# A 2:4-pruned matmul on one Trainium2 core: another opening, with six weight pieces, two load queues and bf16 transposes

## The chip, the core and the metric

The kernel runs on one NeuronCore of a Trainium2 chip. Five engines work side by side, each with its own instruction stream, and wait for one another by semaphores: TensorE (matmuls and their weight loads; PE and PEld in the profile), VectorE (DVE), ScalarE (ACT), GpSimd (POOL) and SyncE (SP). Here SyncE and ScalarE issue the DMAs, each on a queue of its own; the profile counts such issues under SPq and ACTq. Matmul results go to PSUM, which has eight banks, and are read out by VectorE or ScalarE.

The metric is device microseconds of one execution, lowest is best. Before the change the median of 13 runs is 237.35 us.

## What is computed

```python
B, S, D = 16, 512, 1024          # x: (B, S, D), w: (D, D), b: (D), all bf16

def reference(x, w, b):
    N, M = 2, 4
    wg = w.reshape(D // M, M, D)
    mag = jnp.abs(wg)
    order = jnp.argsort(mag, 1)
    thr = jnp.take_along_axis(mag, order[:, M - N:M - N + 1, :], 1)
    wp = (wg * (mag >= thr)).reshape(D, D)
    return jnp.einsum("bsd,df->bsf", x, wp) + b
```

Of every four neighbouring rows of `w`, in each column, the two largest in magnitude are kept and the others set to zero. The pruned matrix then multiplies 8192 tokens of 1024 features, and a bias is added. The product takes 64 token tiles x 8 slices of 128 features x 2 halves of 512 output columns: 1024 matmuls of 128 x 128 by 128 x 512.

## The kernel before

**Two parts.** The first seven token tiles (0 to 6) are multiplied in the "packed" part, while the weights are still being loaded and pruned. The other 57 tiles follow in the "natural" part.

**Packed part.** `w` is held with four neighbouring rows side by side in one partition (`wv`, "(g q m) f -> q g m f"): group g is one half of the 1024 rows, q the partition, m the row of the four. Pruning then compares values of the same partition. The weights are loaded and pruned in seven pieces (L123), given as group and columns: two of 128 columns, three of 256, two of 512. For each piece VectorE runs abs, hi and lo (the larger and smaller of two pairs), t1 and t2, thr (the second largest), mask and mult (`do`, L161); for some pieces ScalarE takes the abs (L159). The product of mult goes to `wp`.

The token tiles must be transposed in the same packed order. `transpose(t, g)` (L192) does this on TensorE for one group ("a" is group 0, "b" group 1): it takes pairs of bf16 values as one fp32 word, so two fp32 transposes move four slices; the identity is fp32. The result lies in PSUM (`psum_t`, two buffers) and `copy_xt` (L201) brings it to SBUF on ScalarE. `mm_piece(t, i)` (L209) multiplies tile t by piece i with four matmuls, m = 0 to 3, into the accumulator of tile t and output half h.

Accumulators come from `psum_o`, six buffers that are handed out in turn; the first goes to the fillers, which are matmuls of zeros into an unused tile (`filler`, L129). When the first output half of a tile is complete, `stage` (L224) copies it to SBUF on ScalarE and so frees its buffer; the second half stays in PSUM until `finish(t)` (L229) adds the bias to both halves on VectorE and issues the store.

**Order.** The order of the packed part is written out by hand as three strings, one for each engine (L249). A token is an operation: T3a transposes tile 3, group 0; C3a copies it; M3.1 multiplies tile 3 by piece 1; F2 is two fillers of 128 columns; S3 stages tile 3; W5 saves piece 5; `abs0` to `mult6` are pruning steps. `run` (L306) emits tokens as soon as what `needs` names has been emitted; each engine then executes its string in order. Ahead of the strings there are six fillers of 512 columns and three of 128.

**Loads.** All loads stand ahead on SyncE's queue, in this order: w of piece 0 and 1 (256 columns, 256 KB), x of tile 0, of tile 1, of tiles 2-3 (group 0; 128 KB for each tile), w of piece 2, x of tiles 4-5, w of piece 3, and so on up to the two 512 KB pieces and the bias.

**Natural part.** The pruned pieces are saved to DRAM (`save`, L183) and read back in natural row order (`reload`, L186) into `wp_nat`. The remaining tokens are loaded in batches by a transposing DMA (`load_batch`, L237). Batch 0 (five tiles) runs all first halves and then all second halves through `nat_group` (L332, matmuls of L334); the other batches interleave the halves (L369). `evac` (L337) adds the bias and `store` (L340) sends the tile out. On SyncE's queue the order after the loads is: four saves, batch 0, reload of half 0, reload of half 1, batches 1 and 2; the saves of the two 512-column pieces are on ScalarE's queue (W5, W6).

Of the kernel before, what the change touches and what calls it, by code (L numbers as in the profile page):

```python
# [10 lines left out]
def kernel(  # L11
# [7 lines left out]
    nc = tc.nc  # L19
    P = 128  # L20
    bf16 = mybir.dt.bfloat16
# [11 lines left out]
    FH = 512  # L33
# [13 lines left out]

    const = ctx.enter_context(tc.tile_pool(name="const", bufs=1))
    dram = ctx.enter_context(tc.tile_pool(name="dram", bufs=1, space=bass.MemoryType.DRAM))
    wtmp = ctx.enter_context(tc.tile_pool(name="wtmp", bufs=2))  # L50
    xtp = ctx.enter_context(tc.tile_pool(name="xtp", bufs=NPK))
    stg = ctx.enter_context(tc.tile_pool(name="stg", bufs=NPK))
    xtb = ctx.enter_context(tc.tile_pool(name="xtb", bufs=3))
# [13 lines left out]
    def pe(i):  # L67
        return seq("pe", i)

    def dve(i):  # L70
        return seq("dve", i)

    def act(i):
        return seq("act", i)
# [3 lines left out]

    zeros = const.tile([P, P], bf16)
    dve(nc.vector.memset(zeros[:], 0.0))  # L80
    spark = const.tile([P, 1], bf16)


    w_sb = const.tile([P, G, 4, Dout], bf16)
# [9 lines left out]
    def load_w(g, c0, c1, eng="sp"):  # L94
        issue(eng, w_sb[:, g, :, c0:c1], wv[:, g, :, c0:c1])

    def load_x(ta, tb, g, eng="sp"):
        xs = const.tile([P, tb - ta, HK], bf16, name=f"x_{ta}_{g}")
        issue(eng, xs[:], xv[:, ta:tb, g * HK:(g + 1) * HK])
        for t in range(ta, tb):  # L100
            x_sb[(t, g)] = xs[:, t - ta, :]


    act(nc.scalar.activation(spark[:], zeros[:, :1], Act.Abs))
    load_w(0, 0, CW)
    load_x(0, 1, 0)
    load_x(1, 2, 0)
    load_x(2, 4, 0)
    load_w(0, CW, FH)
    load_x(4, 6, 0)  # L110
    load_w(1, 0, CW)
    load_x(0, 2, 1)
    load_x(2, 4, 1)
    load_x(6, 7, 0)
    load_w(1, CW, FH)
    load_x(4, 6, 1)
    load_x(6, 7, 1)
    load_w(0, FH, Dout)
    load_w(1, FH, Dout)
    sp(nc.sync.dma_start(bias_sb[:], b.partition_broadcast(P)))  # L120


    pieces = [(0, 0, P), (0, P, CW), (0, CW, FH), (1, 0, CW), (1, CW, FH), (0, FH, Dout), (1, FH, Dout)]  # L123

    ident = const.tile([P, P], fp32)
    make_identity(nc, ident[:])
    warm_ps = psum_o.tile([P, FH], fp32, name="ps")

    def filler(n, rep=1):  # L129
        for _ in range(n):  # L130
            pe(nc.tensor.matmul(warm_ps[:, :rep * P], lhsT=zeros[:],  # L131
                                rhs=zeros[:, None, :].to_broadcast([P, rep, P]), start=True, stop=True))
# [6 lines left out]

    class Piece:  # L140


        def __init__(self, i):
            self.g, self.c0, self.c1 = pieces[i]
            n = self.n = self.c1 - self.c0
            self.w = w_sb[:, self.g, :, self.c0:self.c1]
            self.mag = wtmp.tile([P, 4, FH], bf16, name="mag", bufs=5)[:, :, :n]
            self.hi = wtmp.tile([P, 2, FH], bf16, name="hi")[:, :, :n]
            self.lo = wtmp.tile([P, 2, FH], bf16, name="lo")[:, :, :n]
            self.t1 = wtmp.tile([P, FH], bf16, name="t1")[:, :n]  # L150
            self.t2 = wtmp.tile([P, FH], bf16, name="t2")[:, :n]
            self.thr = wtmp.tile([P, FH], bf16, name="thr")[:, :n]
            self.mask = wtmp.tile([P, 4, FH], bf16, name="mask")[:, :, :n]

        def tt(self, out, a, b_, op):
            dve(nc.vector.tensor_tensor(out, a, b_, op=op))  # L156

        def abs_act(self):
            act(nc.scalar.activation(self.mag, self.w, Act.Abs))  # L159

        def do(self, *steps):  # L161
            magv = self.mag.rearrange("p (a j) f -> p a j f", j=2)
            for step in steps:
                if step == "abs":
                    dve(nc.vector.tensor_single_scalar(
                        self.mag.bitcast(u16), self.w.bitcast(u16), 0x7FFF, op=Alu.bitwise_and))
                elif step == "hi":
                    self.tt(self.hi, magv[:, :, 0, :], magv[:, :, 1, :], Alu.max)
                elif step == "lo":
                    self.tt(self.lo, magv[:, :, 0, :], magv[:, :, 1, :], Alu.min)  # L170
                elif step == "t1":
                    self.tt(self.t1, self.hi[:, 0, :], self.hi[:, 1, :], Alu.min)
                elif step == "t2":
                    self.tt(self.t2, self.lo[:, 0, :], self.lo[:, 1, :], Alu.max)
                elif step == "thr":
                    self.tt(self.thr, self.t1, self.t2, Alu.max)
                elif step == "mask":
                    self.tt(self.mask, self.mag,
                            self.thr[:, None, :].to_broadcast([P, 4, self.n]), Alu.is_ge)
                else:  # L180
                    self.tt(wp[:, self.g, :, self.c0:self.c1], self.w, self.mask, Alu.mult)

    def save(g, c0, c1, eng="sp"):  # L183
        issue(eng, scr_pk[:, g, :, c0:c1], wp[:, g, :, c0:c1])
# [7 lines left out]
    def transpose(t, g):  # L192


        xg = x_sb[(t, g)].bitcast(fp32).rearrange("p (q u) -> p u q", u=2)
        tp = psum_t.tile([P, 2, P], fp32, name="tp")
        for u in range(2):
            pe(nc.tensor.transpose(tp[:, u, :], xg[:, u, :], ident[:]))  # L198
        xpk[(t, g)] = tp

    def copy_xt(t, g):  # L201
        xt = xtp.tile([P, 2, P], fp32, name=f"xt{g}")
        act(nc.scalar.copy(xt[:], xpk[(t, g)][:]))  # L203
        v = xt[:].bitcast(bf16).rearrange("p u (t v) -> p u v t", v=2)
        xpk[(t, g)] = [v[:, m // 2, m % 2, :] for m in range(4)]

    ps_open = {}

    def mm_piece(t, i):  # L209
        g, c0, c1 = pieces[i]  # L210
        h = c0 // FH
        new = (t, h) not in ps_open
        if new:
            ps_open[(t, h)] = psum_o.tile([P, FH], fp32, name="ps")
        ps = ps_open[(t, h)]
        for m in range(4):
            pe(nc.tensor.matmul(ps[:, c0 - h * FH:c1 - h * FH], lhsT=xpk[(t, g)][m],  # L217
                                rhs=wp[:, g, m, c0:c1],
                                start=(new and m == 0), stop=(g == 1 and m == 3),
                                skip_group_check=True))  # L220

    staged = {}
# [14 lines left out]
    def load_batch(bi):  # L237
# [5 lines left out]
        for j in range(nb):  # L243
# [4 lines left out]

    order = {  # L249
        "pe": (  # L250
            "T0a T1a F2 T2a T3a F2 M0.0 M1.0 M2.0 M3.0 T4a T5a M0.1 M1.1 M2.1 M3.1 M4.0 M4.1 T0b "
            "T1b M5.0 M5.1 T2b T6a M0.2 T3b M1.2 M2.2 T4b M3.2 T5b T6b M4.2 M5.2 M0.3 M1.3 M2.3 "
            "M3.3 M4.3 M5.3 M0.4 M1.4 M2.4 M3.4 M4.4 M5.4 M6.0 M6.1 M6.2 M6.3 M6.4 M0.5 M1.5 M2.5 "
            "M3.5 M4.5 M5.5 M0.6 M1.6 M2.6 M3.6 M4.6 M5.6 M6.5 M6.6"
        ),
        "dve": (
            "abs0 hi0 lo0 t10 t20 hi1 thr0 lo1 mask0 t11 mult0 t21 thr1 mask1 mult1 abs2 hi2 lo2 "
            "t12 t22 thr2 mask2 mult2 hi3 lo3 t13 t23 thr3 mask3 mult3 hi4 lo4 t14 t24 thr4 mask4 "
            "mult4 hi5 lo5 t15 t25 thr5 mask5 mult5 hi6 lo6 t16 t26 thr6 mask6 mult6"
        ),  # L260
        "act": (
            "abs1 C0a C1a C2a C3a C4a C5a abs3 C0b C1b C2b C6a abs4 C3b C4b C5b C6b abs5 abs6 S0 S1 "
            "S2 S3 S4 S5 W5 S6 W6"
        ),
    }
    written = set()
    p = {}

    def needs(eng, tok):

        if tok[0] == "C":
            return ["T" + tok[1:]]
        if tok[0] in "TF":
            return []
        if tok[0] == "M":
            t, i = tok[1:].split(".")
            return [f"C{t}{'ab'[pieces[int(i)][0]]}", f"mult{i}"]
        if tok[0] == "S":
            return [f"M{tok[1:]}.{i}" for i in range(5)]
        if tok[0] == "W":  # L280
            return ["mult" + tok[1:]]
        return ["abs" + tok[-1]] if tok[:-1] in ("hi", "mask") else []

    def emit(eng, tok):
        if tok[0] == "T":
            transpose(int(tok[1]), "ab".index(tok[2]))
        elif tok[0] == "F":
            filler(int(tok[1:]))
        elif tok[0] == "C":
            copy_xt(int(tok[1]), "ab".index(tok[2]))  # L290
        elif tok[0] == "M":
            mm_piece(*map(int, tok[1:].split(".")))
        elif tok[0] == "S":
            stage(int(tok[1:]))
        elif tok[0] == "W":
            save(*pieces[int(tok[1:])], eng="act")
        else:
            i = int(tok[-1])
            if i not in p:
                p[i] = Piece(i)  # L300
            if eng == "act":
                p[i].abs_act()
            else:
                p[i].do(tok[:-1])

    def run(queues):  # L306
        while any(queues.values()):
# [6 lines left out]
            assert moved, queues  # L314

    filler(6, 4)
    filler(3)
    run({eng: order[eng].split() for eng in order})
    save(0, 0, CW)
    save(0, CW, FH)  # L320
    save(1, 0, CW)
    save(1, CW, FH)
    load_batch(0)
    reload(0)
    reload(1)
    load_batch(1)
    load_batch(2)
    for t in range(NPK):
        finish(t)


# [76 lines left out]
```

## Time and profile before

| | us |
|---|---|
| median of 13 runs | 237.35 (236.06 to 238.44) |
| the profiled execution, whole | 237.1 |
| its span, first to last instruction | 235.3 |
| TensorE matmuls busy (PE) | 229.6 (98%) |
| weight loads busy (PEld, beside PE) | 113.5 (48%) |
| VectorE busy | 104.8 (45%) |
| ScalarE busy | 16.0 (7%) |
| natural part, interleaved batches (L369) | 175.4 |
| packed products (L217) | 26.3 |
| batch 0 and the last tile (L334) | 21.0 |
| transposes (L198) | 6.1 |

How to read it: a line "L217 PE MATMUL ps<-wp,xt ... x84 | 10.0, 273 | 0.0" is a group of instructions of source line 217, with what they write and read, their number, busy time in us, mean duration of one in ns, and the engine's idle time just before them. Matmuls are pipelined, so the duration of one is longer than the distance to the next; the chain and the records of single instructions give the distance. In the chain of waits a line is a start, a duration (us) and what took it. A row of the table of stages has the granted clock of TensorE as the share of full speed, third from the end.

Landings of the first loads, from the records of single DMAs (issue start, landing, in us):

| load | issued | landed |
|---|---|---|
| w, group 0, columns 0-255 | 0.73 | 3.78 |
| x tile 0, group 0 | 1.48 | 4.10 |
| x tile 1, group 0 | 2.13 | 5.62 |
| x tiles 2-3, group 0 | 2.59 | 6.45 |
| w, group 0, columns 256-511 | 3.07 | 7.30 |
| x tiles 4-5, group 0 | 3.68 | 8.10 |
| w, group 1, columns 0-255 | 4.34 | 9.24 |

### The profile page before, as it was taken

How to read it: one execution, taken by the hardware profiler on the slowest of the kernel's cores; microseconds unless marked ns; L12 is line 12 of the kernel's file. 1: busy time of each engine (PE TensorE's matmuls, PEld its weight loads, DVE VectorE, ACT ScalarE, POOL GpSimd, SP SyncE). 2: the span in 40 equal slices, each digit the busy share in tenths (PEclk: the TensorE clock that was granted, in tenths of full speed). 3: DMA queues.
4: the chain of work that ended last, by engine and by line, in shares of the span. 5: the costliest groups of instructions: out<-in, count | busy, mean ns of one | idle time of the engine just before them, and what ended most of it. 6: DMA issues, size and time to landing. Idle time of an engine off the chain costs nothing.

```text
span 235.3 us, 2830 instructions
## 1 busy us (share of the span) xinstructions
PE 229.6 (98%) x1145; PEld 113.5 (48%) x1165; DVE 104.8 (45%) x182; ACT 16.0 (7%) x28; POOL 0.7 (0%) x6
## 2 busy tenths in 40 slices
PE   6999999999999999999999999999999999999995
PEld 2999444444444444444444444444444444444443
DVE  3899797433433432442443343244234334424424
ACT  4488000000000000000000000000000000000000
POOL 1000000000000000000000000000000000000000
PEclk9999999999999999999999999999999999999999
DMA  4999979999999822893219912497221221222122
GB/s 151 322 350 181 330 247 281 317 280 261 315 240 240 239 92 89 183 286 112 77 59 257 277 47 89 101 254 224 92 84 51 89 89 47 89 89 85 52 89 89
DMA packets 79500, 40.29 MB, mean 171 GB/s; under 512 B 60416, under 2 KB 71936, under 8 KB 79488
## 3 DMA queue, kind: packets, MB, share of 16 engines
q1 hardware_dynamic: 68352, 22.45, 42.4%
q10 hardware_dynamic: 11136, 17.67, 20.9%
q8 instruction: 9, 0.15, 0.3%
q14 instruction: 3, 0.02, 0.0%
HBM read 6.29 MB, written 18.87 MB: 107 GB/s over the span
## 4 chain that ended last, share of the span: by engine, by line
PE 96%; DMA 1%; issue 1%; SPq 1%; DVE 0%
PE ps L369 74%; PE ps L217 11%; PE ps L334 9%; PE tp L198 2%; DMA x<-in_x_dram 1%; SPq L92 1%; PE ps L131 0%; DVE o L338 0%
## 5 line engine op out<-in xcount | busy, mean ns | idle before, releaser
L369 PE MATMUL ps<-wp_nat,xb 128*128 128x512 bf16 x800 | 175.4, 379 | 0.8
L338 DVE TENSOR_TENSOR o<-ps,bias_sb 128x512 bf16<-128x512 f32 (+1 forms) x116 | 74.3, 678 | 120.5 <-PE ps L369 106.4
L369 PEld LDWEIGHTS <-xb 128*128 128x128 bf16 x816 | 79.8, 98 | 96.3
L217 PE MATMUL ps<-wp,xt 128*128 128x256 bf16 (+2 forms) x194 | 26.3, 294 | 0.1
L217 PEld LDWEIGHTS <-xt 128*128 128x128 bf16 x196 | 17.9, 102 | 7.3
L334 PE MATMUL ps<-wp_nat,xb 128*128 128x512 bf16 (+2 forms) x110 | 21.0, 348 | 0.1
L334 PEld LDWEIGHTS <-xb 128*128 128x128 bf16 x112 | 10.3, 98 | 10.7
L198 PE MATMUL tp<-ident,x 128*128 128x128 f32 x28 | 6.1, 339 | 1.0 <-DMA x<-in_x_dram 0.9
L159 ACT ACTIVATE mag<-w_sb 128x1024 bf16<-128x1024 bf16 (+2 forms) x5 | 6.5, 1317 | 1.6 <-DMA w_sb<-in_w_dram 1.6
L231 DVE TENSOR_TENSOR o<-ps,bias_sb 128x512 bf16<-128x512 f32 x7 | 4.8, 684 | 1.9 <-PE ps L217 1.9
L156 DVE TENSOR_TENSOR wp<-w_sb,mask 128x1024 bf16<-128x1024 bf16 (+2 forms) x7 | 5.4, 768 | 0.2
L156 DVE TENSOR_TENSOR mask<-mag,thr 128x1024 bf16<-128x1024 bf16 (+2 forms) x7 | 5.4, 768 | 0.2
L198 PEld LDWEIGHTS tp<-ident,x 128*128 128x128 f32 x28 | 4.4, 207 | 1.9 <-DMA x<-in_x_dram 1.1
L203 ACT COPY xt<-tp 128x256 f32<-128x256 f32 x14 | 4.9, 375 | 5.1 <-PE tp L198 5.1
L131 PE MATMUL ps<-zeros 128*128 128x128 bf16 (+1 forms) x13 | 3.9, 459 | 1.0 <-DVE zeros L80 1.0
L232 DVE TENSOR_TENSOR o<-st,bias_sb 128x512 bf16<-128x512 f32 x7 | 4.8, 681 | 0.0
L156 DVE TENSOR_TENSOR hi<-mag 128x512 bf16<-128x512 bf16 (+2 forms) x7 | 3.2, 461 | 1.4 <-ACT mag L159 1.4
L226 ACT COPY st<-ps 128x512 f32<-128x512 f32 x7 | 3.6, 608 | 0.9 <-PE ps L217 0.9
L156 DVE TENSOR_TENSOR lo<-mag 128x512 bf16<-128x512 bf16 (+2 forms) x7 | 3.2, 457 | 0.0
L131 PEld LDWEIGHTS <-zeros 128*128 128x128 bf16 x13 | 1.7, 143 | 2.8 <-issue 1.7
L156 DVE TENSOR_TENSOR thr<-t,t 128x256 bf16<-128x256 bf16 (+2 forms) x7 | 2.2, 310 | 0.2
L156 DVE TENSOR_TENSOR t<-hi 128x256 bf16<-128x256 bf16 (+2 forms) x7 | 2.1, 305 | 0.0
(11 smaller groups left out, 5.3 us busy)
## 6 DMA issues: line engine op xcount, KB each, us to landing
out_dram<-o ACTq DMA_DIRECT2D x58, 256.0 KB, 3.2
wp_nat<-wp_scratch SPq DMA_DIRECT2D x2, 1024.0 KB, 7.2
x<-in_x_dram SPq DMA_DIRECT2D x5, 256.0 KB, 5.1
out_dram<-o ACTq DMA_DIRECT2D x10, 128.0 KB, 1.7
w_sb<-in_w_dram SPq DMA_DIRECT2D x4, 256.0 KB, 4.6
w_sb<-in_w_dram SPq DMA_DIRECT2D x2, 512.0 KB, 7.2
wp_scratch<-wp SPq DMA_DIRECT2D x4, 256.0 KB, 7.6
wp_scratch<-wp ACTq DMA_DIRECT2D x2, 512.0 KB, 5.4
```

Of the source, the lines that this page charges most:

```text
L131: pe(nc.tensor.matmul(warm_ps[:, :rep * P], lhsT=zeros[:], rhs=zeros[:, None, :].to_broadcast([P, rep, P]), start=True, stop=True))
L156: dve(nc.vector.tensor_tensor(out, a, b_, op=op))
L159: act(nc.scalar.activation(self.mag, self.w, Act.Abs))
L198: pe(nc.tensor.transpose(tp[:, u, :], xg[:, u, :], ident[:]))
L203: act(nc.scalar.copy(xt[:], xpk[(t, g)][:]))
L217: pe(nc.tensor.matmul(ps[:, c0 - h * FH:c1 - h * FH], lhsT=xpk[(t, g)][m], rhs=wp[:, g, m, c0:c1], start=(new and m == 0), stop=(g == 1 an ...
L226: act(nc.scalar.copy(st[:], ps_open.pop((t, 0))[:]))
L231: dve(nc.vector.tensor_tensor(o[:, FH:], ps_open.pop((t, 1))[:], bias_sb[:, FH:], op=Alu.add))
L232: dve(nc.vector.tensor_tensor(o[:, :FH], staged.pop(t)[:], bias_sb[:, :FH], op=Alu.add))
L334: pe(nc.tensor.matmul(ps, lhsT=xt[:, kt, :], rhs=wp_nat[:, kt, c0:c1], start=(kt == 0), stop=(kt == KT - 1)))
L338: dve(nc.vector.tensor_tensor(o[:, c0:c1], ps, bias_sb[:, c0:c1], op=Alu.add))
L369: pe(nc.tensor.matmul(pss[h][:], lhsT=xt[:, kt, :], rhs=wp_nat[:, kt, h * FH:(h + 1) * FH], start=(kt == 0), stop=(kt == KT - 1)))
```

## The change

- **Pieces.** Six instead of seven: four of 256 columns and two of 512. The two 128-column pieces are one piece, 0. Its mask and mult, and its products, are split by rows: "y" is m = 2, 3 and "x" is m = 0, 1, and y goes first.
- **Loads.** The table-loading activation on ScalarE runs three times on 128 columns. Then ScalarE's queue issues x (group 0) of tile 6 and of tiles 4-5. SyncE's queue starts with the first weight piece, then x of tiles 2-3, the second piece, tile 6's group 1, and the rest in a new order, with tile 0's group 0 last but one among x and w.
- **Transposes.** Four bf16 transposes for a block instead of two fp32 ones; the identity is bf16; the copy still moves 256 words of 32 bits to a partition.
- **Pruning in place.** t1, t2, thr and mask overwrite hi, lo and mag, and every piece has its own buffers.
- **Order.** New strings: eight 128-column fillers ahead instead of three, F5, F6 and F7 between the first five transposes, tiles in the order 5, 4, 6, 2, 3, 1, 0, the last products M5.5 to M3.5. `needs` names more. The finishes follow in the order 2, 0, 3, 1, 6, 5, 4. The saves of the 512-column pieces (W5, W4) stand at the end of ScalarE's string.

```diff
-    spark = const.tile([P, 1], bf16)
+    spark = const.tile([P, P], bf16)
...
-    act(nc.scalar.activation(spark[:], zeros[:, :1], Act.Abs))
-    load_w(0, 0, CW)
+    load_w(0, 0, 256)
+    for _ in range(3):
+        act(nc.scalar.activation(spark[:], zeros[:], Act.Abs))
+    load_x(6, 7, 0, "act")
+    load_x(4, 6, 0, "act")
+    load_x(2, 4, 0)
+    load_w(0, 256, 512)
+    load_x(6, 7, 1)
+    load_x(1, 2, 0)
+    load_w(1, 256, 512)
+    load_x(2, 4, 1)
+    load_w(1, 0, 256)
+    load_x(4, 6, 1)
+    load_w(0, 512, 1024)
+    load_x(0, 2, 1)
     load_x(0, 1, 0)
-    load_x(1, 2, 0)
-    load_x(2, 4, 0)
-    load_w(0, CW, FH)
...
+    load_w(1, 512, 1024)
...
-    pieces = [(0, 0, P), (0, P, CW), (0, CW, FH), (1, 0, CW), (1, CW, FH), (0, FH, Dout), (1, FH, Dout)]
-
-    ident = const.tile([P, P], fp32)
+    pieces = [(0, 0, 256), (0, 256, 512), (1, 0, 256), (1, 256, 512), (0, 512, 1024), (1, 512, 1024)]
+
+    ident = const.tile([P, P], bf16)
...
+            elif step == "mask":
+                self.tt(self.mag[:, ms, :], self.mag[:, ms, :],
+                        thr[:, None, :].to_broadcast([P, n, self.n]), Alu.is_ge)
+            else:
+                self.tt(wp[:, self.g, ms, self.c0:self.c1], self.w[:, ms, :], self.mag[:, ms, :], Alu.mult)
...
-        xg = x_sb[(t, g)].bitcast(fp32).rearrange("p (q u) -> p u q", u=2)
-        tp = psum_t.tile([P, 2, P], fp32, name="tp")
-        for u in range(2):
-            pe(nc.tensor.transpose(tp[:, u, :], xg[:, u, :], ident[:]))
+        xg = x_sb[(t, g)].rearrange("p (q m) -> p m q", m=4)
+        tp = psum_t.tile([P, 4, P], bf16, name="tp")
+        for m in range(4):
+            pe(nc.tensor.transpose(tp[:, m, :], xg[:, m, :], ident[:]))
...
-        xt = xtp.tile([P, 2, P], fp32, name=f"xt{g}")
-        act(nc.scalar.copy(xt[:], xpk[(t, g)][:]))
+        xt = xtp.tile([P, 4, P], bf16, name=f"xt{g}")
+        act(nc.scalar.copy(xt[:].bitcast(fp32), xpk[(t, g)][:].bitcast(fp32)))
...
         "pe": (
-            "T0a T1a F2 T2a T3a F2 M0.0 M1.0 M2.0 M3.0 T4a T5a M0.1 M1.1 M2.1 M3.1 M4.0 M4.1 T0b "
-            "T1b M5.0 M5.1 T2b T6a M0.2 T3b M1.2 M2.2 T4b M3.2 T5b T6b M4.2 M5.2 M0.3 M1.3 M2.3 "
-            "M3.3 M4.3 M5.3 M0.4 M1.4 M2.4 M3.4 M4.4 M5.4 M6.0 M6.1 M6.2 M6.3 M6.4 M0.5 M1.5 M2.5 "
-            "M3.5 M4.5 M5.5 M0.6 M1.6 M2.6 M3.6 M4.6 M5.6 M6.5 M6.6"
+            "T6a F5 T5a T4a F6 T3a T2a F7 M5.0y M4.0y M6.0y M2.0y M5.0x M3.0x T6b T1a M6.0x M3.0y "
+            "M4.0x M2.0x M1.0y M1.0x T3b T2b M6.1 M4.1 M3.1 T4b M1.1 M5.1 T5b M2.1 M6.3 M3.3 M4.3 "
+            "T1b T0b M5.3 M2.3 M1.3 M3.2 M6.2 M5.2 T0a M4.2 M2.2 M1.2 M0.0y M0.1 M0.2 M0.3 M0.0x "
+            "M2.4 M3.4 M1.4 M0.4 M5.4 M4.4 M5.5 M2.5 M1.5 M4.5 M6.4 M0.5 M6.5 M3.5"
         ),
         "dve": (
...
+            "abs0 hi0 lo0 t10 t20 thr0 mask0y mask0x mult0y abs1 mult0x hi1 lo1 t11 t21 thr1 mask1 "
+            "mult1 lo3 hi3 t23 t13 thr3 mask3 mult3 lo2 hi2 t22 t12 thr2 mask2 mult2 lo4 hi4 t24 "
+            "t14 thr4 mask4 mult4 hi5 lo5 t25 t15 thr5 mask5 mult5"
         ),
         "act": (
-            "abs1 C0a C1a C2a C3a C4a C5a abs3 C0b C1b C2b C6a abs4 C3b C4b C5b C6b abs5 abs6 S0 S1 "
-            "S2 S3 S4 S5 W5 S6 W6"
+            "C6a C5a C4a C2a C3a C6b C1a abs3 C3b abs2 C2b C4b C5b abs4 C1b abs5 C0a S5 C0b S1 S4 "
+            "S6 S2 S0 S3 W5 W4"
...
-    filler(3)
+    filler(8)
...
-    for t in range(NPK):
+    for t in (2, 0, 3, 1, 6, 5, 4):
         finish(t)
```

## The prediction

> **What bounds the kernel now.** I read the chain of waits first, as shares and then in order of time up to 15 us, to see which engine sets the end and where it does not.
>
> ```profile
> PE 96%; DMA 1%; issue 1%; SPq 1%; DVE 0%
> PE ps L369 74%; PE ps L217 11%; PE ps L334 9%; PE tp L198 2%; DMA x<-in_x_dram 1%; SPq L92 1%; PE ps L131 0%; DVE o L338 0%
> ...
> 2.13 3.48 DMA x<-in_x_dram
> 5.62 0.04 issue
> 5.66 0.70 PE tp L198 x2
> 6.36 0.21 PE ps L131 x2
> ...
> 7.89 1.71 PE ps L217 x16
> 9.60 0.54 PE tp L198 x4
> 10.14 1.34 PE ps L217 x24
> ```
>
> From 5.66 us to the last matmul (the records of single instructions put its end at 232.64) TensorE never stops for more than 0.05 us. Whatever is not TensorE work from there on is hidden. The end can move in three ways: dense work starts at another time than 5.66, the dense stretch holds other work or a new stall, or its beginning runs at another speed. The last is visible above: 16 matmuls of 128 columns take 1.71 us (107 ns each), and later 24 of them take 1.34 us (56 ns). The groups of TensorE by form, up to 36 us, say the same:
>
> ```profile
> L217 PE MATMUL ps<-wp,xt 128*128 128x512 bf16 x54 | 12.1, 379 | 0.1
> L217 PE MATMUL ps<-wp,xt 128*128 128x256 bf16 x84 | 10.0, 273 | 0.0
> L198 PE MATMUL tp<-ident,x 128*128 128x128 f32 x28 | 6.1, 339 | 1.0 <-DMA x<-in_x_dram 0.9
> L131 PE MATMUL ps<-zeros 128*128 128x512 bf16 x6 | 2.7, 630 | 1.0 <-DVE zeros L80 1.0
> ```
>
> A 512-column filler at the start takes 630 ns, a 512-column matmul later 379. The table of stages gives a granted clock of 1.00 in every microsecond, so its first microseconds must not be trusted: the clock's records begin at 9.67 us, and there the spacing halves. I read it as half speed up to 9.67 us. Dense TensorE work had by then run for 4.0 us; before that it had stood still from 4.05 to 4.24 and from 4.91 to 5.66.
>
> Last, VectorE's row for a 256-column piece, since the change makes such a piece the first:
>
> ```profile
> 7.47 0.42 DVE L165 TENSOR_SCALAR mag<-w_sb 128x1024 uint16<-128x1024 uint16 x1
> ...
> 9.45 0.69 DVE L156 TENSOR_TENSOR mask<-mag,thr 128x1024 bf16<-128x1024 bf16 x1
> 10.17 0.69 DVE L156 TENSOR_TENSOR wp<-w_sb,mask 128x1024 bf16<-128x1024 bf16 x1
> ```
>
> **The unit of account.** At 9.98 us the kernel has six transposed blocks and 16 short matmuls (0.89 us at 56 ns) behind it, and 232.64 - 9.98 = 222.66 us of dense full-speed work ahead. For the changed kernel let T be the time at which its first real matmul (M5.0y) starts, counted at full clock; a half-speed stretch of real work after it adds half its length to T. I sum what is then left.
>
> *Packed matmuls.* Before: 56 of 128 columns, 84 of 256, 56 of 512, at spacings of 55.9, 109.2 and 215.8 ns in the records: 3.13 + 9.17 + 12.08 = 24.38 us, less the 0.89 done, 23.49. After: 112 of 256 and 56 of 512: 12.23 + 12.08 = 24.31. Net +0.82. The halves of piece 0 keep the same matmuls.
>
> *Transposes.* Before, eight blocks of two fp32 transposes are left; in the chain's pieces and the records they take 2.1 us. After, nine blocks of four bf16 ones are left (five precede M5.0y). No row shows a bf16 transpose. Nearest is the bf16 matmul of that shape, 55.9 ns: 9 x 4 x 55.9 = 2.0 us, net -0.1. The other bound is the fp32 spacing, 118 ns: 4.2 us, net +2.1. I take the first, since the matmul has the same type and the same moving width, and keep the second for the range. The evacuation stays one 256-word ScalarE copy of 0.37 us.
>
> *A new wait at the hand-over.* Six accumulators rotate. In the new order the first matmul group behind the packed part (L334) takes the accumulator of tile 3's second half, and M3.5 is the last packed product. So that group waits until finish(3) has read it: 0.20 us from the end of a group's stream to its eviction's start (39.04 to 39.24 in the records), 0.69 us eviction, 0.06 us back to TensorE (as from the zeros' memset to the first filler): 0.95 us with TensorE idle. Before, that group took tile 1's accumulator, evicted 3 us earlier. Queued behind on VectorE are the finishes of tiles 1, 6, 5, 4 at 1.2 us each; their accumulators are wanted every 1.73 us, so nothing further is late. Low bound 0, if buffers are handed out otherwise.
>
> Sum: end = T + 222.66 + 0.82 - 0.1 + 0.95 = T + 224.3. It equals 232.64 at **T = 8.3**. All depends on T.
>
> **T.** *Loads.* Before, the third load of SyncE (x of tile 1, issued 2.13) landed only at 5.62 and held TensorE. Now tiles 6, 5 and 4 come by ScalarE's queue, behind a table load (0.74 to 2.02) and three activations. Whether the issues wait for these no row shows directly. For not: a semaphore instruction of ScalarE's sequencer ran at 16.77, inside an activation that lasted from 16.10 to 18.01, so the sequencer runs ahead of its engine. Then the issues fall at about 1.1 and 1.8 us and, with the 2.6 us that x of tile 0 took from issue to landing, tile 6 lands near 3.9 and tiles 4-5 near 5.0. For waiting: issues at 2.6 and 3.2, and with 2.6 to 3.5 us (the two first x loads) tile 6 lands at 5.2 to 6.1. I take the first, and keep both.
>
> *TensorE.* Six fillers of 427 and eight of 107 ns from 0.99 end at 4.37; T6a to 4.80; F5 to 5.33; T5a and T4a follow: with early loads TensorE does not stop. If a full busy stretch of 3.4 to 4 us frees the clock, as 5.66 to 9.67 did, it comes between 4.4 and 7.5, I take 6. Left at 5.33 are 2 + 2 blocks (0.85 us each pair at 107 ns) and F6, F7 (0.64, 0.75): 3.1 us, 0.67 of it slow, the rest halved: 6.0 + 1.2 = 7.2, with 0.2 for the wait of T3a on C5a.
>
> *VectorE.* w of piece 0 is again first, 3.78. By the rows above the mask starts 1.98 after abs, 5.78; two half masks at a 0.33 spacing (512 elements, as mask0 at 5.35), then mult0y from 6.5 to 6.93. So M5.0y can start at 7.0, or 7.2 if the ScalarE loads take bandwidth from the first piece. **T = 7.4.**
>
> *Does it stay dense?* VectorE: abs1 and mult0x to 7.7, then 2.94 us for each 256-column piece: mult1 10.5, mult3 13.5, mult2 16.4; 4.95 for a 512-column one (18.05 to 23.0): mult4 21.3. TensorE from T = 7.4 asks for mult1 at 10.9, mult3 at 14.0, mult2 at 17.1, mult4 at 21.7. Loads: by the cumulative bytes of the landings before (1.28 MB at 8.1, 2.4 MB at 12.7), the second halves of tiles 4-5 land near 12.3, asked for at 12.2. Every margin is under 1 us, so I add 0.2 for small stalls, and T below 7 would bring nothing more. The saves, reloads and the batch's transposing load have the same predecessors; the reload of the second half had 2.9 us to spare, and the later save of piece 4 (now behind S3 on ScalarE, beside piece 5's, about 3.3 us later) still precedes the last save it waits for anyway. In-place pruning changes no shape: 0.
>
> **Sum.** Span change: 7.4 - 8.3 + 0.2 = -0.7. The profiled execution took 237.10 us (span 235.3), the median of the runs is 237.35; the forecast stands on both, 236.4 and 236.65: **236.5 us**, own range 235.9 to 236.85.
>
> **The skill against it.** "TensorE: Matmul & The Clock Gate", Part 4: PE-mode transpose, says that a transpose does not count as busy for the clock's gate. Here the clock rose after a stretch in which 1.2 of 3.4 us were transposes, which does not exclude the rule; by it the new start, with more transposes, would stay slow until after 9 us, which is the first rival's time. "DMA: Bandwidth & Descriptors", section Issuing engines are not separate DMA queues, says that a second issuing engine saves only issue time; the record of this case (0.4 to 0.7 us for each issue) agrees that this much is there to save. By it alone tile 6 would gain one or two issues, which early issue needs.
>
> **Rivals.** (1) *Slower: the clock stays low.* If tile 6 lands at 5.2 or later, TensorE stands from 4.37 on, the window is broken as it was before, and the 4.05 us of slow transposes and fillers run in full: T = 5.1 + 4.05 + half of the slow matmuls (about 0.3) = 9.4, end +1.1, **238.2** (237.9 to 239). It decides from about T6a at 4.8. For: before, two gaps of 0.94 us together did the same. Against: the sequencer running ahead. Chance 0.29. (2) *The gain is eaten*: VectorE or a load falls behind by 0.5 to 1 us (mult4, or x for T4b), **237.2**; for it, margins under 1 us; against, VectorE's idle 0.73 and 0.65 us before the fourth and the sixth piece's work go. 0.14. (3) *bf16 transposes at 118 ns*: +2.2, **238.7**; 0.06. (4) *No hand-over wait*, **235.6**; for it, only that buffers could rotate otherwise; 0.05. The forecast has 0.46.
>
> **Numbers.** About 0.2%, 0.47 us, is what runs of this kernel can tell from no change. Faster: the forecast's 0.46 less its upper edge, with (4): 0.50. Same: (2) and edges, 0.16. Slower: (1), (3): 0.34. The range 235.7 to 238.4 takes in (2), most of (4) and the nearer part of (1).
>
> **What would show it.** Right: tile 6 landed by 4.3; TensorE without a gap from 1 to 8 us; spacings of 56 ns by 7.5; M5.0y at 7.0 to 7.6; one TensorE idle of about 0.95 us released by finish(3)'s eviction, just before L334's counterpart. Wrong: a gap after the first fillers, 107 ns spacings past 8.5, transposes spaced above 70 ns, or waits on mult4.

## The result and the profile after

The changed kernel takes 240.85 us (median of 11 runs, 239.9 to 242.03), the kernel before 237.16 us in the runs beside it: ratio 1.0158, 95% interval 1.0141 to 1.0175. The change costs about 3.7 us. The forecast was 236.5 us, range 235.7 to 238.4, with a chance of 0.34 for slower. Of each kernel's runs, those over 1.5% above its fastest are left out of all medians, ranges and ratios; below, that concerns seven runs of three kernels.

The profiled execution took 239.9 us, the fastest of the eleven, with a span of 238.1. Its chain of waits, the shares by line and then the first 16 us in order of time (start, duration, what):

```profile
PE ps L395 74%; PE ps L220 10%; PE ps L360 9%; DMA x<-in_x_dram 2%; PE tp L195 2%; PE ps L132 1%; ACT L106 1%; ACT spark L106 0%; DVE o L364 0%; ACTq L92 0%
...
2.04 0.32 ACT spark L106
2.35 0.02 issue
2.38 0.32 ACT spark L106
2.69 0.02 issue
2.72 0.31 ACT spark L106
3.03 0.09 ACTq L92
3.12 0.03 issue
3.15 5.41 DMA x<-in_x_dram
8.56 0.05 issue
8.60 1.04 PE tp L195 x8
9.64 0.64 PE ps L132 x6
10.28 0.85 PE tp L195 x8
11.14 0.75 PE ps L132 x7
11.88 1.66 PE ps L220 x12
13.54 0.45 PE tp L195 x8
13.99 1.31 PE ps L220 x12
```

Before, the chain entered TensorE at 5.66 us and stayed there. Now it enters at 8.60, and what stands ahead is new: the three activations, one behind the other, then ScalarE's issue of x for tiles 4-5 at 3.15, and its landing 5.41 us later. From 8.60 to 11.88 TensorE does four transposed blocks and 13 fillers, and no product. Fillers run at 107 ns (0.64 us for 6) and the first 12 products at 138 ns on average; the next 12 run at 109. Eight bf16 transposes take 1.04 and 0.85 us at first and 0.45 later, 56 ns each.

TensorE's timeline has the two gaps, ended by x for tile 6 and x for tiles 4-5:

```profile
0.99 3.60 PE L132 MATMUL ps<-zeros 128*128 128x512 bf16 x14 [0.99 <-DVE zeros L80]
6.53 0.62 PE L195 MATMUL tp<-ident,x 128*128 128x128 bf16 x4 [1.95 <-DMA x<-in_x_dram]
6.95 0.74 PE L132 MATMUL ps<-zeros 128*128 128x128 bf16 x5
8.60 1.04 PE L195 MATMUL tp<-ident,x 128*128 128x128 bf16 x8 [0.92 <-DMA x<-in_x_dram]
```

and ScalarE's timeline says when those loads went out:

```profile
0.74 1.28 ACT L106 ACT_TABLE_LOAD   x1 [0.74 <-PEq L418]
2.04 0.99 ACT L106 ACTIVATE spark<-zeros 128x128 bf16<-128x128 bf16 x3
2.72 0.88 ACTq L92 DMA_DIRECT2D x<-in_x_dram  x2
```

The first issue falls on 2.72 us, the moment at which the third activation starts. Three activations of 0.32 us that follow one another only when the one before has ended (2.04, 2.38, 2.72) are a chain, not a pipeline. The landings, from the records of single DMAs:

| load | queue | issued | landed |
|---|---|---|---|
| w piece 0 | SyncE | 0.74 | 3.83 |
| x tiles 2-3 | SyncE | 1.48 | 5.22 |
| w piece 1 | SyncE | 2.13 | 7.57 |
| x tile 6 | ScalarE | 2.72 | 6.49 |
| x tile 6, group 1 | SyncE | 2.74 | 7.78 |
| x tiles 4-5 | ScalarE | 3.15 | 8.56 |
| x tile 1 | SyncE | 3.40 | 8.37 |

Tiles 4-5, wanted second, land last of the seven. These seven loads are 1.4 MB, tiles 4-5 included, and three of the others (tiles 2-3, tile 6's group 1, tile 1) are wanted only after 9 us. The clock's records begin at 12.46 us here (9.67 before); that is where the spacing of the products changes.

**The account closes.** The prediction's sum, without its hand-over term, puts the last matmul at T + 222.66 + 0.82 - 0.10 = T + 223.38, T being the first product's start counted at full clock. T6b started at 13.38 behind 12 products of 109.2 ns, so T = 12.07 and the end 235.45. Measured: 235.43. This holds for the profiled execution; the median lies 0.95 us above it, and no trace shows what the other ten runs lost. (The profile of the kernel with another order of finishes, below, has the same opening and T = 12.67, so T itself moves by some tenths.)

### The profile page after: what moved, and what is told of

It reads as the page before. It is cut to its first block, busy times and chain, and to the rows that moved or that the text cites. A ratio compares the mean times of both kernels' runs of the same rounds, so it can differ in the third digit from the quotient of the medians.

```text
span 238.1 us, 2853 instructions
## 1 busy us (share of the span) xinstructions
PE 230.5 (97%) x1164; PEld 114.5 (48%) x1184; DVE 104.4 (44%) x177; ACT 16.0 (7%) x29; POOL 0.7 (0%) x6
## 4 chain that ended last, share of the span: by engine, by line
PE 95%; DMA 2%; ACT 1%; issue 1%; DVE 0%; ACTq 0%
PE ps L395 74%; PE ps L220 10%; PE ps L360 9%; DMA x<-in_x_dram 2%; PE tp L195 2%; PE ps L132 1%; ACT L106 1%; ACT spark L106 0%; DVE o L364 0%; ACTq L92 0%
## 5 line engine op out<-in xcount | busy, mean ns | idle before, releaser
L220 PE MATMUL ps<-wp,xt 128*128 128x256 bf16 (+1 forms) x166 | 25.7, 310 | 0.1
L220 PEld LDWEIGHTS <-xt 128*128 128x128 bf16 x168 | 16.4, 99 | 7.7
L195 PE MATMUL tp<-ident,x 128*128 128x128 bf16 x56 | 5.7, 251 | 2.9 <-DMA x<-in_x_dram 2.9
L132 PE MATMUL ps<-zeros 128*128 128x128 bf16 (+1 forms) x32 | 6.1, 372 | 1.0 <-DVE zeros L80 1.0
L195 PEld LDWEIGHTS <-x 128*128 128x128 bf16 x56 | 4.7, 124 | 3.5 <-DMA x<-in_x_dram 3.4
L155 ACT ACTIVATE mag<-w_sb 128x1024 bf16<-128x1024 bf16 (+1 forms) x4 | 6.0, 1491 | 0.0
L152 DVE TENSOR_TENSOR wp<-w_sb,mag 128x1024 bf16<-128x1024 bf16 (+2 forms) x7 | 5.4, 767 | 0.2
L152 DVE TENSOR_TENSOR mag<-mag,hi 128x1024 bf16<-128x1024 bf16 (+2 forms) x7 | 5.3, 767 | 0.2
L132 PEld LDWEIGHTS <-zeros 128*128 128x128 bf16 x32 | 3.7, 147 | 2.6 <-issue 1.6
L152 DVE TENSOR_TENSOR lo<-mag 128x512 bf16<-128x512 bf16 (+1 forms) x6 | 3.1, 509 | 4.2 <-ACT mag L155 4.2
L152 DVE TENSOR_TENSOR hi<-mag 128x512 bf16<-128x512 bf16 (+1 forms) x6 | 3.1, 508 | 0.0
```

The costliest lines, as they stand in the source:

```text
L132: pe(nc.tensor.matmul(warm_ps[:, :rep * P], lhsT=zeros[:], rhs=zeros[:, None, :].to_broadcast([P, rep, P]), start=True, stop=True))
L155: act(nc.scalar.activation(self.mag[:], self.w, Act.Abs))
L195: pe(nc.tensor.transpose(tp[:, m, :], xg[:, m, :], ident[:]))
```

## The experiments

All times are medians in us; the ratio is to the kernel before, run beside it, with its 95% interval. T is found as above (the start of T6b less 1.31).

### ScalarE's loads ahead of the activations

```diff
-    for _ in range(3):
-        act(nc.scalar.activation(spark[:], zeros[:], Act.Abs))
     load_x(6, 7, 0, "act")
     load_x(4, 6, 0, "act")
+    for _ in range(3):
+        act(nc.scalar.activation(spark[:], zeros[:], Act.Abs))
```

> The changed kernel with ScalarE's two x loads ahead of the three activations instead of behind them. My theory: the activations wait for one another (same tile) and hold ScalarE's queue until 2.7 us, so x of tiles 4-5 lands behind loads that are not needed yet (8.56) and TensorE's fourth and fifth tile start at 8.60. With the issues at about 0.75 and 1.4 us, tile 6 lands at 4.0 to 4.5 and tiles 4-5 at 5.0 to 6.2; the first real matmul then stands, counted at full clock, at 7.6 to 9.3 instead of 12.07: 235.4 to 237.3 us against 240.85, ScalarE's queue being the whole of the loss. Rival (bandwidth): the two loads share the DMA engines with w and land no earlier than 7.5 whatever their issue; then over 239.5 us.

236.0 (four runs), ratio 0.9953 (0.9936 to 0.9969): faster than the kernel before. Issues at 0.73 and 1.16, tile 6 landed at 3.04 and tiles 4-5 at 5.58. T = 8.37, last matmul at 231.75, where the sum puts it. Not TensorE but the weights set T here: the two loads took bandwidth from w piece 0, which landed at 5.21 instead of 3.83, and the first product waited 0.82 us for its mult:

```profile
8.37 1.47 PE L220 MATMUL ps<-wp,xt 128*128 128x256 bf16 x12 [0.82 <-DVE wp L152]
```

The bandwidth rival falls.

### The same loads on SyncE's queue

```diff
-    load_x(6, 7, 0, "act")
-    load_x(4, 6, 0, "act")
+    load_x(6, 7, 0)
+    load_x(4, 6, 0)
     load_x(2, 4, 0)
```

> The changed kernel with the two x loads on SyncE's queue, right behind the first weight piece (tile 6, tiles 4-5, tiles 2-3), the activations as they are. If only the order of the bytes counts, tile 6 lands near 4.1 and tiles 4-5 near 6.0 us, as the second and third place of that queue gave before (4.10, and 6.45 for 640 KB); TensorE has gaps of 0.2 and 0.7 us before them, so the clock stays at half until about 9.4: first real matmul at 9.2 to 9.6 counted at full clock, 237.0 to 237.6 us. If a second queue by itself were worth something, this would be slower than the run with ScalarE's loads first by over 0.5 us.

236.15 (six runs), ratio 0.9962 (0.9950 to 0.9974), 0.85 us below the expected range: the landings were 4.28 and 5.61, TensorE had almost no gap, and the clock rose at 6.97 already. Its interval overlaps the one above, so no worth of a second queue by itself is seen. That agrees with the rule of the Trainium skill weighed in the prediction ("DMA: Bandwidth & Descriptors", section Issuing engines are not separate DMA queues).

### The gaps filled, the loads left late

```diff
-            "T6a F5 T5a T4a F6 ...
+            "T6a F20 T5a T4a F6 ...
...
-    filler(8)
+    filler(30)
```

> The changed kernel with 30 instead of 8 fillers ahead and 20 instead of 5 between T6a and T5a, so that TensorE has no gap while it waits for the same late loads. My theory: the clock rises when a stretch of some 3.4 us is busy throughout, so it rises between 4.4 and 7.8 instead of 12.46; T5a still starts at 8.6, then transposes and fillers run at full speed: first real matmul at 10.3 to 10.6, 238.1 to 238.5 us, 2.4 us less than 240.85. Rival (transposes and fillers of zeros do not count for the clock, as the rule of the notes has it for transposes): the clock still rises after 11 us and the time stays at 240 or more.

240.08, ratio 1.0131 (1.0107 to 1.0154). The clock rose at 6.00 instead of 12.46 us and T was 10.40, as expected: the clock follows TensorE's gaps. But the time hardly moved, and the expected 238.1 to 238.5 was missed; 1.49 us were given back at 55.64, in this row of TensorE's timeline:

```profile
36.72 17.43 PE L360 MATMUL ps<-wp_nat,xb 128*128 128x512 bf16 x79
55.64 19.60 PE L395 MATMUL ps<-wp_nat,xb 128*128 128x512 bf16 x88 [1.49 <-DMA xb<-in_x_dram]
```

Batch 1's transposing load landed at 55.60. In the changed kernel it landed at 53.78, 1.9 us before it was wanted (55.66), so it was hidden there. It is a second limit close behind the first, and the prediction had added nothing for it.

### Both: SyncE's queue and 12 fillers

```diff
-            "T6a F5 T5a ...
+            "T6a F12 T5a ...
```

(on top of the second experiment)

> Both: the two x loads on SyncE's queue and 12 fillers instead of 5 between T6a and T5a. My theory: T5a at 6.1, clock at full speed by 7.8 at the latest, first real matmul at 7.6 to 8.2 counted at full clock: 235.4 to 236.2 us, faster than the kernel before by 1 to 1.7 us, if VectorE and the later loads keep up; they may cost 0.3 to 0.8 us. Rival (the clock needs real matmuls): 238 or more.

236.21 (235.76 to 237.36), ratio 0.9967 (0.9947 to 0.9987). T = 7.74 in the profile, but that execution, the slowest of the ten, lost 1.43 us at batch 1's load. The clock had been early without the extra fillers as well, and they bring nothing here that the runs can tell.

### W4 ahead of W5, in the two filled kernels

```diff
-            "... S6 S2 S0 S3 W5 W4"
+            "... S6 S2 S0 S3 W4 W5"
```

> The filled kernel (30 and 20 fillers, the late loads as they are) with the saves W4 and W5 in the order of their pruning, W4 ahead of W5. The filled run had its first real matmul at 10.40 at full clock, 1.67 us earlier than the changed kernel, and lost 1.49 us of it again at 54 to 55.6 us, where TensorE waited for the transposing load of batch 1. My theory: that load stands on SyncE's queue behind the reload of the second half, which waits for both saves; W4 waited for the last pruned piece only because W5 stood ahead of it. With W4 first it is issued at about 26 instead of 30 us, the reload goes out 1 to 1.4 us earlier, and the wait shrinks to 0 to 0.5: 238.3 to 239.2 us instead of 240.08. Rival: the DMA engines are full then and the load lands when it lands; 239.7 or more.

> The kernel with the x loads on SyncE's queue and 12 fillers, with W4 ahead of W5. It lost 1.43 us at the same load of batch 1 in its profile (first real matmul at 7.64). Theory: without that wait 235.4 to 236.0 us instead of 236.21, and runs that scatter less than 235.8 to 237.4. Rival: unchanged, 236.2 or more.

With the late loads: 239.4, ratio 1.0097 (1.0054 to 1.0139), single runs from 238.5 to 241.2, which is not clear of the kernel without the exchange (1.0107 to 1.0154). With SyncE's loads: 236.31, ratio 0.9955 (0.9939 to 0.9971), single runs from 235.8 to 238.4: the rival. In the profile of the second, its slowest run, W5 still waits for mult5 and the reload waits for W5: it went out at 33.19 instead of 33.97, and batch 1's load landed later, at 54.15 against 53.09, 2.1 us after it was wanted:

```profile
54.20 11.18 PE L395 MATMUL ps<-wp_nat,xb 128*128 128x512 bf16 x51 [2.10 <-DMA xb<-in_x_dram]
```

So the theory fell there. What makes that load take 13.9 us (before) to 20.5 us (here) from issue to landing stays open.

### Three tiles for the three activations

```diff
-    spark = const.tile([P, P], bf16)
+    sparks = [const.tile([P, P], bf16, name=f"spark{i}") for i in range(3)]
...
-    for _ in range(3):
-        act(nc.scalar.activation(spark[:], zeros[:], Act.Abs))
+    for i in range(3):
+        act(nc.scalar.activation(sparks[i][:], zeros[:], Act.Abs))
```

> The changed kernel with the three activations writing three tiles instead of one; nothing else moves. My theory: ScalarE's x loads were issued at 2.72 us because the third activation waits on a semaphore for the second, and the queue's sequencer stands at that wait; without it the sequencer runs ahead and issues them between 1.0 and 2.2 us. Then tile 6 lands at 3.8 to 5.0 and tiles 4-5 at 5.5 to 7.0, and the time is 235.8 to 238. Rival (the queue waits until the activations have run): issue at 2.7 us again, 240.4 to 241.2 us.

**235.48, ratio 0.9936 (0.9911 to 0.9962)**, the lowest median of all. The only difference to the changed kernel is which bytes the activations write. In the trace of the changed kernel the second and the third activation each wait for a semaphore that the activation before them raises; with three tiles neither waits for one. The waits are there because each activation overwrites what the one before wrote. The sequencer (the part of an engine that reads its instruction stream) stands at such a wait, and the DMA issues behind it with it. Without the waits, ScalarE's and TensorE's timelines are:

```profile
0.74 1.28 ACT L106 ACT_TABLE_LOAD   x1 [0.74 <-PEq L418]
0.98 0.88 ACTq L92 DMA_DIRECT2D x<-in_x_dram  x2
2.03 0.71 ACT L106 ACTIVATE spark<-zeros 128x128 bf16<-128x128 bf16 x3
```

```profile
0.99 3.60 PE L132 MATMUL ps<-zeros 128*128 128x512 bf16 x14 [0.99 <-DVE zeros L80]
4.38 0.63 PE L195 MATMUL tp<-ident,x 128*128 128x128 bf16 x4
4.81 0.74 PE L132 MATMUL ps<-zeros 128*128 128x128 bf16 x5
5.34 0.80 PE L195 MATMUL tp<-ident,x 128*128 128x128 bf16 x8
5.97 0.50 PE L132 MATMUL ps<-zeros 128*128 128x128 bf16 x6
6.38 0.66 PE L195 MATMUL tp<-ident,x 128*128 128x128 bf16 x8
6.87 0.55 PE L132 MATMUL ps<-zeros 128*128 128x128 bf16 x7
7.29 1.47 PE L220 MATMUL ps<-wp,xt 128*128 128x256 bf16 x12
```

The DMAs go out while the table is still being loaded, and the three activations overlap (0.71 us for all). There is not one gap from 0.99 us on. The clock's record begins at 5.72, T = 7.29 (forecast 7.4), and the last matmul ends at 230.66, the sum's 230.67. The two profiled executions, 239.90 and 235.10 us, differ by 4.80 us, their T by 4.78. Of ten runs, seven lie between 235.1 and 235.8, three between 236.3 and 237.6.

### The finishes in the order 2, 3, 0

```diff
-    for t in (2, 0, 3, 1, 6, 5, 4):
+    for t in (2, 3, 0, 1, 6, 5, 4):
         finish(t)
```

> The changed kernel with the finishes in the order 2, 3, 0, 1, 6, 5, 4. The prediction had a wait of 0.95 us at the hand-over (L360's first group behind the eviction of tile 3, the last product); the profile shows none. If accumulators are handed on in the order in which they are released by the program, the first group took tile 0's; with tile 3 second it takes tile 3's and TensorE stands 0.8 to 1.0 us before L360. If they are handed out in a fixed turn, nothing changes: no gap.

A single run, so its row and not its time (241.45) counts. The first line is the changed kernel, the others this one:

```profile
38.39 6.85 PE L360 MATMUL ps<-wp_nat,xb 128*128 128x512 bf16 x31
...
24.84 14.32 PE L220 MATMUL ps<-wp,xt 128*128 128x256 bf16 x75
39.94 17.43 PE L360 MATMUL ps<-wp_nat,xb 128*128 128x512 bf16 x80 [0.78 <-DVE o L234]
```

The wait of the prediction appears: 0.78 us behind the modelled end of the last product, 0.94 behind the end of its stream (a 512-column product's 379 ns less the 216 of its spacing). T = 12.67 here, and T + 223.38 + 0.94 = 236.99; the last matmul ended at 236.98. So accumulators are handed on in the order of the finishes, and "in turn" in the description of the kernel before is to be read in this way; the changed kernel's order, with tile 0 second, avoids the wait.

### Batch 1's load earlier, the reload on ScalarE's queue

```diff
-    def reload(h):
+    def reload(h, eng="sp"):
...
-        sp(nc.sync.dma_start(wp_nat[:, :, fs], scr_nat[:, :, fs]))
+        issue(eng, wp_nat[:, :, fs], scr_nat[:, :, fs])
...
     load_batch(0)
     reload(0)
-    reload(1)
     load_batch(1)
+    reload(1, "act")
     load_batch(2)
```

(on top of the three tiles)

> The three-tile kernel with the reload of the second half moved from SyncE's to ScalarE's queue, behind W5 and W4, and batch 1's transposing load therefore right behind the first reload on SyncE's queue. In the three-tile runs most lay at 235.1 to 235.3 and three at 236.3 to 237.6. My theory: the slow ones waited for batch 1's load, which stood some 8 us behind the reload's wait for the saves (issued 33.2, landed 49.6, wanted at 50.9); other kernels' profiles show that wait at 1.4 to 4.1 us. With the load issued near 24.5 it lands before 46 and all runs come to 235.0 to 235.5. Rival: the earlier transposing load takes the bandwidth of the saves and reloads, and TensorE waits for the second half's reload (wanted at 42.2) instead: 235.8 or more.

244.94, ratio 1.0336 (1.0298 to 1.0374): the rival, and at a much higher price than it had. TensorE's timeline, and the table of stages around the wait (the granted clock is the third number from the end):

```profile
39.83 2.75 PE L360 MATMUL ps<-wp_nat,xb 128*128 128x512 bf16 x12
50.37 2.32 PE L360 MATMUL ps<-wp_nat,xb 128*128 128x512 bf16 x5 [7.79 <-DMA wp_nat<-wp_scratch]
```

```profile
40.00:46.90 6.90, 2.58 (x12) 0.98 (x10) 1.87 (x4) 0.00 (x0) 0.00 (x0) 1.00 1.24 277
46.90:53.70 6.80, 3.11 (x7) 1.20 (x9) 1.39 (x2) 0.00 (x0) 0.00 (x0) 0.50 1.11 354
```

With batch 1's transposing load beside them throughout (24.69 to 40.07), and batch 2's from 33.65 on, the saves W5 and W4 took 12.1 and 12.9 us. In the three-tile kernel, where batch 0's load lay beside only their first 1.1 and 0.4 us, they took 5.0 and 5.8. The reload took 10.3 us instead of 7.0. TensorE stood for 7.79 us, and the clock fell to half for 6.8 us (46.93 to 53.76). The reload's wait on SyncE's queue, which looks like a hindrance, holds the transposing loads back from the saves.

### The kernel before, gaps filled

```diff
-            "T0a T1a F2 T2a ...
+            "T0a F8 T1a F2 T2a ...
...
-    filler(3)
+    filler(5)
```

> The kernel before with five fillers instead of three ahead of T0a and eight more between T0a and T1a, so that TensorE has no gap from 1 us on. My theory of the clock: it rises before 7.8 instead of 9.67 us, and the first 16 products run at full speed; 1.3 us is won at 10 us, of which the late products of piece 5 (mult5 ends at 23.0, then wanted at 22.2) give back up to 0.8: 236.3 to 236.9 us against 237.2. Rival (the clock does not follow the gaps): 237.1 to 237.5.

236.44, ratio 0.9971 (0.9951 to 0.9992), as expected. The clock's record begins at 6.04 instead of 9.67. Ten fillers of zeros win 0.8 us for the kernel before (0.2 to 1.2 by the interval).

### The kernel before with bf16 transposes alone

```diff
-    ident = const.tile([P, P], fp32)
+    ident = const.tile([P, P], bf16)
...
-        for u in range(2):
-            pe(nc.tensor.transpose(tp[:, u, :], xg[:, u, :], ident[:]))
+        for m in range(4):
+            pe(nc.tensor.transpose(tp[:, m, :], xg[:, m, :], ident[:]))
```

> The kernel before with the bf16 transposes alone (four for a block, bf16 identity, the same copy). At the 56 ns spacing that the changed kernel's profile shows, the eight blocks behind 9.98 us cost 1.8 instead of 2.1 us; the six slow ones cost the same 0.43 us each: 236.8 to 237.1 us, a gain of 0.1 to 0.4 that may not be told from no change. Rival (118 ns each): 238.5 or more.

236.6, ratio 0.9969 (0.9952 to 0.9985). The gain is 0.4 to 1.1 us, the upper end of what was expected or more. How much of it is the transposes' spacing is not shown: in the two profiles the last matmul ends at the same time (232.64 and 232.63), with the clock at full speed for good from 10.45 here and from 9.67 before. The rival of 118 ns is out.

### Batch 2's load later

```diff
-    load_batch(2)
...
-        load_batch(bi + 3)
+        if bi:
+            load_batch(bi + 3)
...
-                        store("act", tb + j, outs[j])
+                        store("sp" if j == 2 else "act", tb + j, outs[j])
+                        if j == 2:
+                            load_batch(2)
+            load_batch(3)
```

(on top of the three tiles; batch 3's load moves too, so that it stays behind batch 2's)

> The three-tile kernel with batch 2's transposing load moved on SyncE's queue behind the store of batch 0's third tile (issued near 48.4 us instead of 46.2), so that batch 1's load is alone for longer; in the kernel with W4 ahead of W5 it ended 8.6 us after its issue did, with batch 2's load beside it. My theory: that is what scatters the three-tile runs (most at 235.1 to 235.3, three at 236.3 to 237.6); without it all lie at 235.0 to 235.5, median 235.2. Rivals: batch 2 then comes late itself (wanted at 64.7, landing at 60 to 64): 235.6 to 237; or the scatter comes from elsewhere and stays: 235.4 to 235.7, single runs to 237.6.

237.2, ratio 1.0026 (0.9998 to 1.0054), single runs from 235.8 to 239.1: slower than the three-tile kernel, and nearest to the first rival. In the profile, its best run, the load, issued at 48.92, landed at 65.30, 0.3 us late. Batch 2's load has no such time to give away; why single runs of the three-tile kernel lie 1 to 2 us higher stays open.

## Why the prediction was wrong

**The step that failed: the issue of ScalarE's loads.** The prediction named both ways, "whether the issues wait for these no row shows directly", and took the first because a semaphore instruction had run inside an activation. That a sequencer runs ahead of its engine is right: the three-tile run issues at 0.98, inside the table load. What was missed is in the code and not in the profile before: the three activations write the same tile, so each waits for the one before, and the sequencer did not run past these waits (first issue at 2.72). It needed no trace, only the question which buffer each new instruction writes. The three-tile run shows it, with nothing else moved: 5.4 us between its median and the changed kernel's, 4.8 between the profiled executions.

**The bound for that case was too low as well.** For late issues (rival 1, chance 0.29) the prediction had tile 6 at 5.2 to 6.1 us, T = 9.4, 238.2 us, at most 239. Measured: tile 6 at 6.49, T = 12.07, 240.85 us. It priced the first of the two loads alone. The second was in flight beside the five SyncE loads of the table, and later ones, and took 5.41 us (4.42 and 3.88 when it was issued at 1.16 and 1.41), so T5a started at 8.60 where that case has 6.06 (5.1 and 0.96 for T6a and F5). The remaining four blocks and 13 fillers then cost their full slow 3.3 us, and the first products 0.2 more. Bytes had been summed for the later loads, not for these.

**Right, by the other steps.**
- Work behind T: +0.82 for the products, -0.1 for the transposes. The end is T + 223.38 to 0.02 us in the changed kernel, with ScalarE's loads first, and with three tiles.
- bf16 transposes at the spacing of a bf16 matmul: 56 ns.
- The schedule with early loads: T = 7.4 forecast, 7.29 in the three-tile run. (The fillers' spacings add up to 4.41 us, where the prediction has 4.37; TensorE went on at 4.38.) That kernel takes 235.48 us, 1.0 us under the forecast, because neither the hand-over wait of 0.95 nor the 0.2 for small stalls came.
- The clock: half until a stretch without gaps has passed. The filled kernels raise it at 6.00 and 6.04, at 12.46 and 9.67 without. The moment is not fixed by the kernel alone: two kernels with the same opening, the three tiles and batch 2's load later, have 5.72 and 4.84.

**Wrong in size or place.** The hand-over wait was priced right (0.95; 0.94 where it was provoked) and put where it does not occur: 0 in the changed kernel, as rival (4) had it with a chance of 0.05. The prediction took the accumulators to rotate in a fixed turn. "The saves, reloads and the batch's transposing load have the same predecessors" was true and not enough: batch 1's load landed 5.1 us before it was wanted in the kernel before, 1.9 in the changed and 1.3 in the three-tile kernel. It goes out 1.0 and 1.3 us later against the time at which it is wanted, and takes 16.1 and 16.4 us instead of 13.9. Kernels with a faster start ran into it.

**Left open: whether transposes count for the clock.** On the rule of the Trainium skill that transposes do not count as busy for the clock in the same way (TensorE: Matmul & The Clock Gate, Part 4: PE-mode transpose): the three-tile clock rose with transposes in some 0.8 of the 3.4 us before. That is no decision; no run here had transposes alone.

## What to carry over

Ask of a warm-up or delay instruction placed ahead of a DMA issue on the same queue what it waits for: here repeated writes to one scratch tile made a chain of waits, and the loads behind them were late; without the waits the loads went out at 0.98 us. When a load is moved, sum the bytes that pass before or beside it up to its landing; here its own size and issue told little. And a change that wins at the start should be followed to the next thing with under 2 us to spare (here a load 45 us later), or the gain is given back there.

## Not expected of the hardware

- The clock moves in steps of 3.41 us in these records. In the kernel before with bf16 transposes its records give full speed from 3.62 to 7.04, half to 10.45, then full. The table of stages of that run (clock third from the end) shows the middle:

```profile
3.70:7.00 3.30, 1.38 (x18) 0.88 (x16) 2.98 (x14) 1.38 (x3) 0.00 (x0) 1.00 0.89 245
7.10:10.40 3.30, 3.30 (x35) 3.30 (x32) 3.13 (x10) 1.12 (x3) 0.00 (x0) 0.50 1.00 308
```

  TensorE was busy for 1.38 of 3.30 us in the first of these stretches, and the clock was taken back for the next, in which it was busy throughout.
- One late load cost twice in the run with the earlier batch 1: 7.79 us of standing still, and then 3.4 us of work at half speed (half speed was granted from 46.93 to 53.76, and TensorE worked again from 50.37).
- A 512 KB save took 5.0 us with a transposing load beside its first 1.1 us alone, and 12.1 us with one beside it throughout and a second one beside its last 4.9 us.
